# Attention with gated MLP on one core: six heads per Q/K group, matmuls of one kind in pairs, and work moved between engines

## Chip, cores, metric

One core of one Trainium2 chip. The metric is the device time of one execution in microseconds (us), taken as the median of several executions of the same program. The profiles come from one execution each; their spans are about 2 us shorter than the device time.

## The reference

The sequence has 2048 tokens of width 640; there are 32 heads of only 20 columns.

```python
g = sigmoid((x * gate_w).sum(-1, keepdims=True))
# a: full attention
qkv = x @ wqkv                                   # 2048 x 1920
p = softmax(q @ k.T * 20 ** -0.5)                # per head, 2048 x 2048
a = (p @ v).reshape(2048, 640) @ wo
# b: MLP with "mish"
h = x @ w1 + b1                                  # 2048 x 1536
b = (h * tanh(log(1 + exp(h)))) @ w2
out = g * a + (1 - g) * b
```

Inputs, weights and the result are bf16.

## The kernel before

The program is written engine by engine. Each engine works through its own queue and waits on semaphores; an instruction that waits holds up those queued behind it, and this is what the argument turns on: in the run with the multiply on VectorE, the copy of a finished Q product stood behind a multiply that waited 7.12 us.

The first stretch computes V, the gate, Q and K (transposed, `QT` and `KT`) and the whole MLP. A list of events fixes the order: "h" is one hidden tile of the MLP (128 of 1536 features, 512 tokens), "q" and "k" are one Q or K product, "b" is the down-projection of 512 tokens. Q and K come in groups of four heads; each head is padded from 20 to 32 columns, and GpSimd copies the padded weights into `PAD`.

```python
QKP = PB[4]                                      # one PSUM bank for Q and K
# TensorE, for an event "q" or "k":
if qk_last is not None:
    pk, pi = qk_last
    pe.wait_ge(s_qfree if pk == "q" else s_kfree, pi + 1)
for ft in range(NFT):                            # 5 matmuls
    pe.matmul(QKP[:, 0:512], PAD[gb][:, side, ft, :], XT[:, ft, qc*512:(qc+1)*512], ...)
# VectorE:  "q": tensor_copy(QT..., QKP)    4th "h": wait for tanh, multiply HB*UB -> ACTT, four times
# ScalarE:  "k": copy(KT..., QKP)           4th "h": flush_batch(), see below     "b": copy the block out
...
def flush_batch():                               # ScalarE, four tiles
    for t in pending: HB = Identity(h + b1); UB = Exp(h + b1)
    for t in pending: UB = Ln(UB + 1)            # table load before
    for t in pending: UB = Tanh(UB)              # table load before
```

The second part is attention. For each of two halves of the queries (1024 each) it does 512 steps; a step is one head and 128 keys. S is the score product into one of three PSUM buffers `T`, exp moves it to `ETS`, V accumulates into `OTACC`. S matmuls use 128x128 weights. V matmuls use 128x21 weights and put each head of a group of four into its own 32 rows of `OTACC` (a column tile).

```python
ND = 3                                           # buffers T and ETS
# ScalarE
act.wait_ge(s_s, s + 1)
if s >= ND: act.wait_ge(s_v, s - ND + 1)
act.activation(ETS[b], T[b], AF.Exp, scale=SCALE).then_inc(s_e, 1)
# TensorE
def emit_S(s):  # wait s_e >= s-ND+1; two matmuls 128x512 with KTZ (128x128)
def emit_V(s):  # wait s_e >= s+1;   two matmuls 128x512 with V_all (128x21), tile_position=(0, 32*j)
for k0 in range(ND): emit_S(base + k0)
for k in range(steps_per_qr):
    emit_V(base + k)
    if k + ND < steps_per_qr: emit_S(base + k + ND)
```

`KTZ` holds the K rows of one head with all other rows zero, so that S of one head can use all 128 rows of `QT`. After each group of 64 steps VectorE copies `OTACC` out, and the next group's first V waits for that.

The softmax here doesn't subtract the row's maximum and nothing guards it: scores larger than these inputs give would overflow.

Of the kernel before, what the change touches and what calls it, by code (L numbers as in the profile page):

```python
# [10 lines left out]
P = 128  # L11
D = 640
# [3 lines left out]
NG = 8  # L16
NFT = D // P
# [5 lines left out]
def bass_gated_mix__softmax_full_mha__dense_activation_mish__prompt_kernel(  # L23
# [30 lines left out]
    def sem(name):  # L54
        return st.enter_context(nc.semaphore(name))

    V_all = st.enter_context(nc.sbuf_tensor("V_all", [P, NKT, H, 21], BF16))
    QT = st.enter_context(nc.sbuf_tensor("QT", [P, NG, S], BF16))
    KT = st.enter_context(nc.sbuf_tensor("KT", [P, NG, S], BF16))
# [45 lines left out]
    s_ktz = [sem("s_ktz0"), sem("s_ktz1")]  # L105
# [26 lines left out]
    def pool_chain_inc(ins, other=None, other_val=None):  # L132
# [4 lines left out]
        else:  # L137
# [10 lines left out]
    ctxQ = ExitStack()  # L148
    WQKV = ctxQ.enter_context(nc.sbuf_tensor("WQKV", [P, NFT, 1920], BF16, side="right"))
    PAD = [ctxQ.enter_context(nc.sbuf_tensor(f"PAD{i}", [P, 2, NFT, P], BF16, side="right"))  # L150
           for i in range(2)]
# [5 lines left out]
    QKP = PB[4]  # L157
# [5 lines left out]
    items = [(g, qc) for g in range(NG) for qc in range(NQC)]  # L163
# [24 lines left out]
    with nc.Block() as blk:  # L188
        @blk.sync
        def _(sp):  # L190
            for ft in range(NFT):
                sp.dma_start_transpose(XT[:, ft, :], x_ap[:, ft * P:(ft + 1) * P]).then_inc(s_xt, 16)
            sp.dma_start(W1[:, :, :], B_w1.rearrange("(ft p) c -> p ft c", p=P)).then_inc(s_w1, 16)
            sp.wait_ge(s_qfree, NITEMS)
            sp.wait_ge(s_kfree, NITEMS)
# [11 lines left out]
        @blk.vector  # L207
        def _(dve):
            ins = dve.memset(V_all[:, :, :, 0:1], 1.0)
            dve_chain_inc(ins, s_dve_init, 1)  # L210
            dve.wait_ge(s_misc, 16 * N_MISC)
            dve.tensor_copy(B1F[:, :], B1T[:, :]).then_inc(s_b1f, 1)

        @blk.gpsimd
        def _(pool):
            pool.wait_ge(s_wq, 16)
            for g in range(NG):
                b = g % 2
                if g >= 2:
                    pool.wait_ge(s_kready, NQC * (g - 1))  # L220
                pool_chain_wait(pool)
                ins = pool.memset(PAD[b][:, :, :, :], 0.0)
                pool_chain_inc(ins)
                todo = []
                for side in range(2):
                    off = side * D
                    for j in range(4):
                        c0 = off + (4 * g + j) * DH
                        todo.append((side, j, c0))
                for idx, (side, j, c0) in enumerate(todo):  # L230
                    pool_chain_wait(pool)
                    ins = pool.tensor_copy(PAD[b][:, side, :, 32 * j:32 * j + DH],
                                           WQKV[:, :, c0:c0 + DH])
                    if idx == len(todo) - 1:
                        pool_chain_inc(ins, s_pad[b], (g // 2) + 1)
                    else:
                        pool_chain_inc(ins)
# [46 lines left out]
        ctxQ.close()  # L284
        W2 = ctxB.enter_context(nc.sbuf_tensor("W2", [P, NFC, D], BF16, side="right"))

        @blk.sync
        def _(sp):
            sp.dma_start(W2[:, :, :], B_w2.rearrange("(fc p) c -> p fc c", p=P)).then_inc(s_w2, 16)

        @blk.tensor
        def _(pe):
# [4 lines left out]
            for ev in events:  # L297
# [13 lines left out]
                elif kind in ("q", "k"):  # L311
                    i = ev[1]
                    g, qc = items[i]
                    gb = g % 2
                    if qc == 0 and kind == "q":
                        pe.wait_ge(s_pad[gb], (g // 2) + 1)
                    if qk_last is not None:
                        pk, pi = qk_last
                        pe.wait_ge(s_qfree if pk == "q" else s_kfree, pi + 1)
                    side = 0 if kind == "q" else 1  # L320
                    ins = None
                    for ft in range(NFT):
                        ins = pe.matmul(QKP[:, 0:512], PAD[gb][:, side, ft, :],  # L323
                                        XT[:, ft, qc * 512:(qc + 1) * 512],
                                        start=(ft == 0), stop=(ft == NFT - 1))
# [19 lines left out]
        @blk.vector  # L345
        def _(dve):
            pending = []

            def flush_batch():
                for t in pending:  # L350
                    tc, fc = divmod(t, NFC)
                    b = t % BK
                    dve.wait_ge(s_mish_act, t + 1)
                    if fc == 0 and tc >= 2:
                        dve.wait_ge(s_bp_ready, TBC * (tc - 1))
                    dve_chain_wait(dve)
                    ins = dve.tensor_tensor(ACTT[tc % 2][:, fc, :], HB[b][:, :], UB[b][:, :], ALU.mult)  # L357
                    dve_chain_inc(ins, s_act_ready, t + 1)
                pending.clear()

            for ev in events:
                kind = ev[0]
                if kind == "q":
                    i = ev[1]
                    g, qc = items[i]
                    dve.wait_ge(s_qready, i + 1)
                    dve.tensor_copy(QT[:, g, qc * 512:(qc + 1) * 512], QKP[:, 0:512]).then_inc(s_qfree, 1)  # L367
                elif kind == "h":
                    pending.append(ev[1])
                    if len(pending) == BK:  # L370
                        flush_batch()
                elif kind == "b":
                    if pending:
                        flush_batch()
            if pending:
                flush_batch()

        @blk.scalar
        def _(act):
# [25 lines left out]
            for ev in events:  # L405
# [5 lines left out]
                elif kind == "k":  # L411
                    i = ev[1]
                    g, qc = items[i]
                    act.wait_ge(s_kready, i + 1)
                    act.copy(KT[:, g, qc * 512:(qc + 1) * 512], QKP[:, 0:512]).then_inc(s_kfree, 1)  # L415
# [16 lines left out]
    ETS = [ctxC.enter_context(nc.sbuf_tensor(f"ETS{i}", [P, 1024], BF16)) for i in range(3)]  # L432
# [6 lines left out]
    KTZ = [[ctxC.enter_context(nc.sbuf_tensor(f"KTZ{b}_{j}", [P, S], BF16)) for j in range(4)]  # L439
           for b in range(2)]  # L440
    T = [ctxC.enter_context(nc.psum_tensor(f"T{i}", [P, 1024], FP32)) for i in range(3)]
    OTACC = ctxC.enter_context(nc.psum_tensor("OTACC", [P, 1024], FP32))
    ND = 3

    steps = []
    for qr in range(NQR):
        for g in range(NG):
            for j in range(4):
                for kt in range(NKT):
                    steps.append((qr, g, j, kt))  # L450
    NS = len(steps)
    assert NS == NSTEPS
    steps_per_qr = NG * 4 * NKT
    wo_v = A_wo.rearrange("(g j r) c -> j r g c", g=NG, j=4, r=DH)

    with nc.Block() as blk2:
        @blk2.vector
        def _(dve):
# [6 lines left out]
            for b in range(2):  # L465
                for j in range(4):
                    dve_chain_wait(dve)
                    ins = dve.memset(KTZ[b][j][:, :], 0.0)  # L468
                    if b == 1 and j == 3:
                        dve_chain_inc(ins, s_cinit, 1)  # L470
                    else:
                        dve_chain_inc(ins)
# [38 lines left out]
        @blk2.scalar  # L511
        def _(act):
            for s, (qr, g, j, kt) in enumerate(steps):
                b = s % ND
                act.wait_ge(s_s, s + 1)
                if s >= ND:
                    act.wait_ge(s_v, s - ND + 1)
                act.activation(ETS[b][:, :], T[b][:, :], AF.Exp, scale=SCALE).then_inc(s_e, 1)  # L518

        @blk2.sync  # L520
        def _(sp):
# [15 lines left out]
            for gi in range(NGRP):  # L537
                gb = gi % 2
                g = gi % NG
                qr = gi // NG  # L540
                if gi >= 2:
                    sp.wait_ge(s_s, (gi - 1) * STEPS_PER_GROUP)
                for j in range(4):
                    sp.dma_start(KTZ[gb][j][32 * j:32 * j + DH, :],  # L544
                                 KT[32 * j:32 * j + DH, g, :]).then_inc(s_ktz[gb], 16)
                if qr >= 1 and g == 1:
                    out_dmas(qr - 1)
                if gi >= 1:
                    pg = gi - 1
# [14 lines left out]
        def _(pe):  # L564
            def emit_S(s):
                qr, g, j, kt = steps[s]
                b = s % ND
                gi = qr * NG + g
                gb = gi % 2
                if s >= ND:  # L570
                    pe.wait_ge(s_e, s - ND + 1)
                if j == 0 and kt == 0:
                    pe.wait_ge(s_ktz[gb], 16 * 4 * (gi // 2 + 1))
                ins = None
                for c in range(2):
                    q0 = qr * 1024 + c * 512
                    ins = pe.matmul(T[b][:, c * 512:(c + 1) * 512],  # L577
                                    KTZ[gb][j][:, kt * P:(kt + 1) * P],
                                    QT[:, g, q0:q0 + 512],
# [3 lines left out]
            def emit_V(s):  # L583
                qr, g, j, kt = steps[s]
                b = s % ND
                h_ = 4 * g + j
# [5 lines left out]
                for c in range(2):  # L592
                    ins = pe.matmul(OTACC[32 * j:32 * j + DH + 1, c * 512:(c + 1) * 512],  # L593
                                    V_all[:, kt, h_, 0:DH + 1],
                                    ETS[b][:, c * 512:(c + 1) * 512],
# [20 lines left out]
            for qr in range(NQR):  # L616
# [5 lines left out]
                for k in range(steps_per_qr):  # L622
                    s = base + k
                    emit_V(s)
                    if k + ND < steps_per_qr:
                        emit_S(s + ND)
# [32 lines left out]
```

## Time and profile before

| | before |
|---|---|
| median of 6 runs | 1607.46 us (1606.52 to 1612.88) |
| first stretch (last MLP block copied out) | 394.7 us |
| setup of attention, to the first S | 18.7 us |
| first half, first S to end of last V | 556.4 us |
| between the halves | 38.4 us |
| second half | 554.5 us |
| after the last V | 42.1 us |

The windows view gives the busy time of each engine in chosen stretches (columns: us of the stretch, busy us and instruction count of TensorE, its weight loads, VectorE, ScalarE and GpSimd, then the granted clock, which is the share of full speed that TensorE was allowed, the DMA share and GB/s). Of the kernel before:

```profile
core 0: us, PE busy (x) PEld busy (x) DVE busy (x) ACT busy (x) POOL busy (x), PEclk, DMA share, GB/s
48.00:234.00 186.00, 114.20 (x433) 42.34 (x434) 30.25 (x53) 76.50 (x123) 20.05 (x54) 0.84 0.00 0
234.00:395.00 161.00, 93.78 (x512) 44.48 (x510) 12.50 (x29) 92.69 (x158) 0.00 (x0) 0.81 0.04 13
395.00:413.00 18.00, 0.00 (x0) 0.00 (x0) 10.46 (x11) 0.00 (x0) 0.00 (x0) 0.57 0.31 64
413.00:970.00 557.00, 550.12 (x2048) 111.60 (x2048) 59.50 (x22) 524.26 (x512) 0.00 (x0) 1.00 0.09 9
```

Two different limits show. From 48 to 234 us no engine is busy all the time and the granted clock is 0.84: engines wait for one another. From 413 to 970 us TensorE and ScalarE both look almost full, and busy time alone can't tell which one is the bound.

For the first stretch, the timeline of the kernel before (start, duration, engine, line; in brackets the idle time of the engine before it and what ended it):

```profile
88.21 1.25 PE L323 MATMUL PB<-XT,PAD 128*128 128x512 bf16 x5 [0.68 <-ACT KT L415]
89.30 1.24 PE L307 MATMUL PB<-XT,W 128*128 128x512 bf16 x5
89.50 0.69 DVE L367 CAST QT<-PB 128x512 bf16<-128x512 f32 x1 [3.28 <-PE PB L323]
90.38 1.24 PE L323 MATMUL PB<-XT,PAD 128*128 128x512 bf16 x5
91.66 0.59 ACT L415 CAST KT<-PB 128x512 bf16<-128x512 f32 x1 [3.50 <-PE PB L323]
...
92.39 1.24 PE L323 MATMUL PB<-XT,PAD 128*128 128x512 bf16 x5 [0.77 <-ACT KT L415]
```

A product, its copy, the next product: only a hidden tile (L307) hides the copy. It is worse when ScalarE is in a batch of four tiles: the K copies wait behind it, and so does TensorE. The waits view from 48 to 234 us has these sums (waiting engine and line, released by, us in total, times, longest):

```profile
PE PB L323 <- ACT KT L415: 43.2, 16, 8.7
PEld PB L323 <- DVE QT L367: 43.1, 31, 11.7
PE PB L323 <- DVE QT L367: 28.5, 23, 11.2
```

The longest waits, 8.7 and 11.2 us, come near the length of a batch: a batch took 11.6 us (four tiles of Identity and Exp, 1.28 us of table load, 2.19 us of Ln, 1.28 us of table load, 2.19 us of Tanh).

For attention, the timeline of TensorE, kernel before (L577 is S, L593 is V; x2 means two matmuls, and durations are modelled, so read the starts):

```profile
700.41 0.60 PE L577 MATMUL T<-QT,KTZ 128*128 128x512 bf16 x2
700.94 0.60 PE L593 MATMUL OTACC<-ETS,V_all 128*21 128x512 bf16 x2
701.48 0.60 PE L577 MATMUL T<-QT,KTZ 128*128 128x512 bf16 x2
702.01 0.60 PE L593 MATMUL OTACC<-ETS,V_all 128*21 128x512 bf16 x2
```

A step is 1.07 us. The starts of single matmuls in the trace tell more. Where matmuls of one kind follow one another the distance is 0.216 us (median of the Q and K products). Within a step it is 0.226 (S to S), 0.309 (S to V), 0.223 (V to V) and 0.312 us (V to S). Nothing released these matmuls late: the exp that V needs had ended 1.0 us earlier. ScalarE's first three exps, which wait for nothing, start 0.92 and 0.90 us apart, but later exps start 1.07 us apart, each 0.04 us after its S has ended. So TensorE is the bound, and 0.19 us of each step is lost at the two changes of kind (the recorded texts call them changes of the tiling mode, or mode changes).

### The profile page before, as it was taken

The page shows a single profiled execution, that of the slowest core. Times are in us where ns is not written, and L with a number is a line of the kernel's source. Part 1 is how long each engine was busy: PE and PEld are TensorE (multiplying, and loading weights), DVE is VectorE, ACT ScalarE, POOL GpSimd, SP SyncE. Part 2 cuts the span into 40 slices and gives each one's busy share as a digit, 9 for nine tenths or more (in the row PEclk, how much of TensorE's full clock was granted, in tenths as well). Part 3 has the DMA queues.
Part 4 walks back from the last instruction along what each step waited for, and adds up shares of the span by engine and source line. Part 5 has one row for each costly group of instructions (what it writes and reads, how often), then busy time and mean ns, then how long its engine had stood idle before and what let it go on. Part 6 is the DMA issues. An engine that isn't in the chain of part 4 may idle for free.

```text
span 1604.7 us, 14101 instructions
## 1 busy us (share of the span) xinstructions
PE 1371.2 (85%) x5536; PEld 346.5 (22%) x5536; DVE 231.0 (14%) x207; ACT 1218.7 (76%) x1306; POOL 26.9 (2%) x76
## 2 busy tenths in 40 slices
PE   4666645556699999999999995999999999999994
PEld 2322212223121121212112122212121221212112
DVE  2211110101102102020210204110102021020205
ACT  0333352781699999999999991899999999999980
POOL 1011100000000000000000000000000000000000
PEclk9978887788799999999999997999999999999997
DMA  6000001000101011010101102001101010110102
GB/s 176 0 1 1 0 1 49 0 1 9 28 1 15 1 16 15 1 15 1 15 2 14 16 1 31 17 1 16 9 7 15 1 15 1 16 15 1 7 1 40
DMA packets 23755, 22.80 MB, mean 14 GB/s; under 512 B 14856, under 2 KB 19080, under 8 KB 23688
## 3 DMA queue, kind: packets, MB, share of 16 engines
q1 hardware_dynamic: 20584, 19.44, 9.2%
q10 hardware_dynamic: 3104, 2.46, 0.5%
q8 instruction: 43, 0.70, 0.2%
q14 instruction: 24, 0.20, 0.0%
HBM read 7.21 MB, written 2.62 MB: 6 GB/s over the span
## 4 chain that ended last, share of the span: by engine, by line
PE 70%; DVE 3%; DMA 1%; issue 0%; SPq 0%; ACT 0%; DVEq 0%
PE OTACC L593 34%; PE T L577 34%; PE T L610 2%; DVE OUNG L483 1%; DMA BCSB<-RTMP 1%; DVE RTMP L487 1%; PE T L612 0%; DVE KTZ L468 0%; ACT ETS L518 0%; DMA KTZ<-KT 0%; SPq L544 0%; DVE WOG L460 0%; SPq L553 0%; SPq L558 0%; DVE DIFF L501 0%
## 5 line engine op out<-in xcount | busy, mean ns | idle before, releaser
L518 ACT ACTIVATE ETS<-T 128x1024 bf16<-128x1024 f32 x1024 | 1048.1, 1024 | 119.2 <-PE T L577 73.9
L577 PE MATMUL T<-QT,KTZ 128*128 128x512 bf16 x2048 | 620.9, 385 | 20.4 <-DMA KTZ<-KT 19.5
L593 PE MATMUL OTACC<-ETS,V_all 128*21 128x512 bf16 x2048 | 616.0, 383 | 12.7 <-DVE OUNG L483 12.2
L577 PEld LDWEIGHTS T<-QT,KTZ 128*128 128x128 bf16 x2048 | 116.9, 97 | 459.4 <-ACT ETS L518 428.6
L593 PEld LDWEIGHTS OTACC<-ETS,V_all 128*21 128x21 bf16 x2048 | 106.0, 90 | 448.6 <-issue 424.9
L323 PE MATMUL PB<-XT,PAD 128*128 128x512 bf16 x320 | 91.7, 423 | 83.0 <-ACT KT L415 43.2
L483 DVE CAST OUNG<-OTACC 128x1024 bf16<-128x1024 f32 x16 | 19.6, 1225 | 862.1 <-PE OTACC L593 862.1
L487 DVE RECIPROCAL RTMP<-OUNG 128x1024 bf16<-128x1024 bf16 x16 | 104.8, 6553 | 0.6
L415 ACT CAST KT<-PB 128x512 bf16<-128x512 f32 x32 | 18.7, 583 | 112.8 <-PE PB L323 112.8
L339 PE MATMUL PB<-W,ACTT 128*128 128x512 bf16 x192 | 59.7, 408 | 44.0 <-ACT BALL L424 35.0
L307 PE MATMUL PB<-XT,W 128*128 128x512 bf16 x240 | 64.3, 418 | 11.2 <-ACT UB L392 10.8
L610 PE MATMUL T<-WOG,OTN 128*128 128x512 bf16 x128 | 39.2, 411 | 36.0 <-DVE OTN L493 36.0
L323 PEld LDWEIGHTS PB<-XT,PAD 128*128 128x128 bf16 x320 | 30.3, 105 | 138.7 <-DVE QT L367 54.8
L423 ACT CAST BALL<-PB 128x512 bf16<-128x512 f32 x16 | 9.3, 583 | 63.4 <-PE PB L341 63.4
L357 DVE TENSOR_TENSOR ACTT<-HB,UB 128x512 bf16<-128x512 bf16 x48 | 20.4, 425 | 164.9 <-ACT UB L402 161.3
L341 PE MATMUL PB<-W,ACTT 128*128 128x128 bf16 x192 | 44.0, 229 | 0.0
L249 PE MATMUL PB<-WQKV,XT 128*128 128x500 bf16 x80 | 23.7, 393 | 22.0 <-DMA XT<-in_A_x_dram 22.0
L367 DVE CAST QT<-PB 128x512 bf16<-128x512 f32 x32 | 22.1, 691 | 106.7 <-PE PB L323 106.7
L339 PEld LDWEIGHTS PB<-W,ACTT 128*128 128x128 bf16 x192 | 19.9, 104 | 73.7 <-ACT BALL L424 38.0
L307 PEld LDWEIGHTS PB<-XT,W 128*128 128x128 bf16 x240 | 25.3, 107 | 46.5 <-issue 12.4
L391 ACT ACTIVATE HB<-PB,B1F 128x512 bf16<-128x512 f32 x48 | 33.7, 702 | 0.7 <-PE PB L307 0.7
L392 ACT ACTIVATE UB<-PB,B1F 128x512 bf16<-128x512 f32 x48 | 34.0, 708 | 0.0
(35 smaller groups left out, 296.9 us busy)
## 6 DMA issues: line engine op xcount, KB each, us to landing
KTZ<-KT SPq DMA_DIRECT2D x64, 80.0 KB
BCSB<-RTMP SPq DMA_DIRECT2D x64, 64.0 KB, 5.6
W<-in_B_w_dram SPq DMA_DIRECT2D x2, 1920.0 KB, 8.8
out_dram<-OUTT SPq DMA_DIRECT2D x16, 160.0 KB, 1.8
WQKV<-in_A_wqkv_dram ACTq DMA_DIRECT2D x1, 2400.0 KB, 9.5
WOG<-in_A_wo_dram SPq DMA_DIRECT2D x4, 200.0 KB
B1T<-in_B_b_dram ACTq DMA_DIRECT2D x12, 0.2 KB, 7.8
XT<-in_A_x_dram SPq DMA_TRANSPOSE x5, 5.3
```

Source lines behind the costliest of these rows:

```text
L307: ins = pe.matmul(hp[:, 0:TCW], W1[:, ft, fc * P:(fc + 1) * P], XT[:, ft, tc * TCW:(tc + 1) * TCW], start=(ft == 0), stop=(ft == NFT - 1))
L323: ins = pe.matmul(QKP[:, 0:512], PAD[gb][:, side, ft, :], XT[:, ft, qc * 512:(qc + 1) * 512], start=(ft == 0), stop=(ft == NFT - 1))
L339: pe.matmul(BPa[:, 0:512], ACTT[tc % 2][:, fc, tbl * P:(tbl + 1) * P], W2[:, fc, 0:512], start=(fc == 0), stop=(fc == NFC - 1))
L341: ins = pe.matmul(BPb[:, 0:128], ACTT[tc % 2][:, fc, tbl * P:(tbl + 1) * P], W2[:, fc, 512:640], start=(fc == 0), stop=(fc == NFC - 1))
L391: act.activation(HB[b][:, :], hp[:, 0:TCW], AF.Identity, bias=B1F[:, fc:fc + 1], scale=1.0)
L392: act.activation(UB[b][:, :], hp[:, 0:TCW], AF.Exp, bias=B1F[:, fc:fc + 1], scale=1.0).then_inc(s_hp_actdone, 1)
L483: ins = dve.tensor_copy(OUNG[:, :], OTACC[:, :])
L487: ins = dve.reciprocal(RTMP[:, :], OUNG[:, :])
L518: act.activation(ETS[b][:, :], T[b][:, :], AF.Exp, scale=SCALE).then_inc(s_e, 1)
L577: ins = pe.matmul(T[b][:, c * 512:(c + 1) * 512], KTZ[gb][j][:, kt * P:(kt + 1) * P], QT[:, g, q0:q0 + 512], start=True, stop=True)
L593: ins = pe.matmul(OTACC[32 * j:32 * j + DH + 1, c * 512:(c + 1) * 512], V_all[:, kt, h_, 0:DH + 1], ETS[b][:, c * 512:(c + 1) * 512], star ...
L610: pe.matmul(T[b][:, 0:512], OTN[:, g, tbl * P:(tbl + 1) * P], WOG[:, g, 0:512], start=(g == 0), stop=(g == NG - 1))
```

## The change

The intent: Q and K in groups of six heads without padding (fewer products, no `PAD`), separate PSUM banks for Q and K, all Q/K copies on VectorE, the multiply on GpSimd, W2 loaded early; in attention, S and V in pairs with six exp buffers.

```diff
-    QKP = PB[4]
+    QKB = {'q': PB[4], 'k': PB[5]}
...
-                    if qk_last is not None:
-                        pk, pi = qk_last
-                        pe.wait_ge(s_qfree if pk == "q" else s_kfree, pi + 1)
+                    if i >= 1:
+                        pe.wait_ge(s_qfree if kind == "q" else s_kfree, i)
+                    c0 = (0 if kind == "q" else D) + g6 * 6 * DH
...
-                        ins = pe.matmul(QKP[:, 0:512], PAD[gb][:, side, ft, :],
+                        ins = pe.matmul(QKB[kind][0:mc, 0:512], WQKV[:, ft, c0:c0 + mc],
...  # VectorE: both copies, nothing else
-                    dve.tensor_copy(QT[:, g, qc * 512:(qc + 1) * 512], QKP[:, 0:512]).then_inc(s_qfree, 1)
+                    dve.tensor_copy((QT if kind == "q" else KT)[0:mc, g6, qc * 512:(qc + 1) * 512],
+                                    QKB[kind][0:mc, 0:512]).then_inc(s_qfree if kind == "q" else s_kfree, 1)
...  # the multiply, in GpSimd's own queue
-                    ins = dve.tensor_tensor(ACTT[tc % 2][:, fc, :], HB[b][:, :], UB[b][:, :], ALU.mult)
+                pool.tensor_tensor(ACTT[tc % 2][:, fc, :], HB[b][:, :], UB[b][:, :],
+                                   ALU.mult).then_inc(s_act_ready, 1)
...  # ScalarE no longer copies K
-                    act.copy(KT[:, g, qc * 512:(qc + 1) * 512], QKP[:, 0:512]).then_inc(s_kfree, 1)
...  # attention: 6 instead of 8 zeroed KTZ, one K load per head; six ETS
-                if s >= ND:
-                    act.wait_ge(s_v, s - ND + 1)
+                if s >= NE:                      # NE = 6
+                    act.wait_ge(s_v, s - NE + 1)
...
-                for k in range(steps_per_qr):
-                    s = base + k
-                    emit_V(s)
-                    if k + ND < steps_per_qr:
-                        emit_S(s + ND)
+                for k in range(0, steps_per_qr, 2):
+                    for kk in (k, k + 1):
+                        if kk + ND < steps_per_qr:
+                            emit_S(base + kk + ND)
+                    for kk in (k, k + 1):
+                        emit_V(base + kk)
```

(Cut: the zeroing of the unused rows of `QT` and `KT`, the index arithmetic of the six-head groups, the K loads, the W2 load.)

## The prediction

> What bounds the kernel now. The windows view and the timeline show three stretches: projections and MLP, 0 to 395 us; setup to the first score matmul at 413.4 us; attention, twice 512 steps of S (2 matmuls), exp, V (2 matmuls), each half followed by about 40 us of normalisation, output projection and store.
>
> Attention is bound by TensorE, not by ScalarE's exp. A step lasts 1.070 us: its matmuls start 0.226 (S to S), 0.309 (S to V), 0.223 (V to V) and 0.312 us (V to S) apart. Between matmuls of one kind (end of the first half; MLP) it is 0.216, so each change between 128x128 and 128x21 matmuls costs about 0.095 us. [...] ScalarE's first three exps, which wait for nothing, start 0.91 us apart; later each starts 0.04 us after its S ends.
>
> The first stretch is bound by a serial chain through one PSUM bank: each Q or K product waits for the copy of the one before (0.69 us on VectorE, 0.59 on ScalarE), and the K copies stand in ScalarE's queue behind a four-tile exp/ln/tanh batch (11.6 us). So 24 hidden tiles take 48 to 248 us, at a granted clock near 0.8.
>
> What the change does.
>
> 1. S,S,V,V order halves the mode changes. Two steps: 2 x 0.31 + 2 x 0.225 + 4 x 0.216 = 1.935 us, 0.967 a step. Saving 0.103 x 1024 = 105 us. Six exp buffers let V lag; exp at 0.91 just fits.
> 2. At the 14 group boundaries inside the halves V waits 0.94 us for the copy of OTACC; one more S pair covers 0.44 of it: 6 us.
> 3. Six heads per Q/K group: 48 products, not 64; separate banks for Q and K; all copies on VectorE; no padding. TensorE should run without waits: 24 x 3 x 1.08 us = 78 us, not 200. ScalarE's 11.6 us a batch fits in TensorE's 13.
> 4. W2 is loaded early: the 9 us wait before the first down-projection goes, but ScalarE's last batch (about 8 us) is exposed instead. First evacuated block at about 135, not 262.6 us; the same 4.28 us cadence; the stretch ends near 270.
> 5. The gating multiply moves to GpSimd. [...] ScalarE reuses a tile each 1.14 us: 0 to 4 us lost.
> 6. Setup: six zeroed KTZ, not eight (2.4 us); first S waits for one copy, not four (about 2 us).
>
> Sum: 125 + 4 + 105 + 6 = 240 us off 1607, plus 3 for a cold clock: 1370 us. Range 1345 to 1398. Faster by over 2%: 0.97; within 2%: 0.02; slower: 0.01.
>
> Signs. Right: S to V and V to S still 0.31 but half as many, step mean 0.967, TensorE never waiting for exp; clock near 1.0 from 48 to 126 us; first evacuated MLP block at 135; attention from 284. Wrong on 1: steps near 1.07, or exps back to back with TensorE waiting for them. Wrong on 3: gaps before Q/K products released by VectorE copies, or tiles waiting for ScalarE.
>
> What could make it wrong: exp in steady state slower than 0.91 us with its second semaphore wait; a multiply on GpSimd over 1.3 us, stalling ScalarE each batch; a clock that stays low in the first stretch; KTZ loads late behind other waits of their queue.

## The result and the profile after

The changed kernel's median is 1365.16 us (8 runs, 1361.86 to 1367.38); the kernel before ran at 1608.64 us (16 runs). The ratio is 0.848, with a 95% interval of 0.8468 to 0.8492. A ratio here is the mean time of one kernel's fast runs over that of the other's fast runs of the same rounds, so not quite the ratio of the medians.

| us, from the traces | before | after | saved | predicted |
|---|---|---|---|---|
| first stretch, to the last MLP block copied out | 394.7 | 271.2 | 123.5 | 125, less 3 for a cold clock |
| setup, to the first S | 18.7 | 14.1 | 4.6 | 4 |
| both halves of attention | 1110.9 | 998.9 | 112.0 | 105 + 6 |
| between and after the halves | 80.5 | 81.2 | -0.7 | 0 |
| span | 1604.7 | 1365.4 | 239.3 | 237 |

(A "cold clock" is a stretch in which TensorE, after a wait, runs below full speed. In the kernel before, after the wait of 9.02 us for W2, a 512-column matmul took 0.43 us to the next start from 257.7 to 260.8 us, and 0.216 from 261.3 us on. That block took 6.15 us to the start of the next one, the later ones 4.28; the predicted 3 us are the author's estimate.) The windows view of the changed kernel:

```profile
48.00:127.00 79.00, 78.63 (x427) 42.82 (x424) 32.99 (x50) 62.77 (x98) 22.46 (x20) 1.00 0.00 1
127.00:271.00 144.00, 94.79 (x513) 45.35 (x511) 1.37 (x2) 88.90 (x152) 31.36 (x28) 0.83 0.00 1
271.00:285.00 14.00, 0.00 (x0) 0.00 (x0) 8.63 (x9) 0.21 (x2) 0.00 (x0) 0.63 0.34 67
285.00:785.00 500.00, 496.65 (x2048) 153.78 (x2048) 59.29 (x21) 494.45 (x512) 0.00 (x0) 1.00 0.11 10
```

The Q/K part is now TensorE work without gaps, 78.63 of 79 us, at full clock. The timeline of the changed kernel there (L299 is a Q or K product, L286 a hidden tile, L329 the copies, L340 the multiply):

```profile
90.12 2.32 PE L299 MATMUL PB<-XT,WQKV 128*120 128x512 bf16 x10
...
91.40 0.69 DVE L329 CAST QT<-PB 120x512 bf16<-120x512 f32 x1 [1.47 <-PE PB L299]
...
92.28 1.24 PE L286 MATMUL PB<-XT,W 128*128 128x512 bf16 x5
92.48 0.69 DVE L329 CAST KT<-PB 120x512 bf16<-120x512 f32 x1 [0.39 <-PE PB L299]
...
93.36 2.32 PE L299 MATMUL PB<-XT,WQKV 128*120 128x512 bf16 x10
93.87 4.49 POOL L340 TENSOR_TENSOR ACTT<-HB,UB 128x512 bf16<-128x512 bf16 x4 [8.45 <-ACT UB L367]
```

A Q and a K product follow each other without a gap (x10), no PE line has a wait in brackets, and the copies and the multiply run beside them. The waits view from 48 to 127 us has no wait of TensorE for a copy any more; the waits that remain are those of engines with time to spare:

```profile
DVE QT L329 <- PE PB L299: 34.8, 23, 2.0
ACT HB L356 <- PE PB L286: 14.1, 9, 2.0
```

TensorE in attention, changed kernel (L545 is S, L562 is V):

```profile
501.24 1.03 PE L562 MATMUL OTACC<-ETS,V_all 128*21 128x512 bf16 x4
502.20 1.04 PE L545 MATMUL T<-QT,KTZ 128*128 128x512 bf16 x4
503.17 1.03 PE L562 MATMUL OTACC<-ETS,V_all 128*21 128x512 bf16 x4
```

Four of a kind, and 1.93 us from one V to the next V for two steps. The distances between starts of single matmuls, from the traces (median us, and how many pairs):

```
            S to S         S to V         V to V         V to S
before      0.226 (1028)   0.309 (1020)   0.223 (1028)   0.312 (1019)
after       0.216 (1538)   0.309 (510)    0.216 (1538)   0.312 (509)
```

The price of a change is the same; there are half as many. At the 14 group boundaries inside the halves the S to V distance was 1.25 us before and is 0.82 us now: the copy of `OTACC` takes 1.225 us in both traces, but two S pairs cover more of it.

### The profile page after: what moved, and what is told of

The parts are those of the page before. It is cut to its first block, busy times and chain, and to the rows that moved or that the text cites. A ratio compares the mean times of both kernels' runs of the same rounds, so it can differ in the third digit from the quotient of the medians.

```text
span 1365.4 us, 13841 instructions
## 1 busy us (share of the span) xinstructions
PE 1230.3 (90%) x5456; PEld 430.8 (32%) x5456; DVE 232.0 (17%) x177; ACT 1141.9 (84%) x1274; POOL 54.0 (4%) x52
## 4 chain that ended last, share of the span: by engine, by line
PE 74%; DVE 4%; DMA 2%; issue 0%; SPq 0%; ACT 0%; DVEq 0%; ACTq 0%
PE OTACC L562 36%; PE T L545 35%; PE T L579 2%; DVE OUNG L452 1%; DMA BCSB<-RTMP 1%; DVE RTMP L456 1%; PE T L581 0%; DVE KTZ L437 0%; DMA out_dram<-OUTT 0%; DVE OUTT L475 0%; DMA KTZ<-KT 0%; DVE DIFF L470 0%; DVE WOG L430 0%; SPq L521 0%; SPq L526 0%
## 5 line engine op out<-in xcount | busy, mean ns | idle before, releaser
L487 ACT ACTIVATE ETS<-T 128x1024 bf16<-128x1024 f32 x1024 | 988.8, 1022 | 62.4 <-PE T L545 62.4
L545 PE MATMUL T<-QT,KTZ 128*128 128x512 bf16 x2048 | 532.5, 383 | 16.7 <-DMA KTZ<-KT 14.9
L562 PE MATMUL OTACC<-ETS,V_all 128*21 128x512 bf16 x2048 | 528.6, 381 | 6.1 <-DVE OUNG L452 6.1
L545 PEld LDWEIGHTS T<-QT,KTZ 128*128 128x128 bf16 x2048 | 158.7, 98 | 358.4 <-ACT ETS L487 212.1
L562 PEld LDWEIGHTS OTACC<-ETS,V_all 128*21 128x21 bf16 x2048 | 148.4, 92 | 349.2 <-ACT ETS L487 214.0
L286 PE MATMUL PB<-XT,W 128*128 128x512 bf16 x240 | 60.5, 400 | 11.2 <-ACT UB L357 10.8
L340 POOL TENSOR_TENSOR ACTT<-HB,UB 128x512 bf16<-128x512 bf16 x48 | 53.8, 1153 | 186.7 <-ACT UB L367 186.7
L299 PE MATMUL PB<-XT,WQKV 128*120 128x512 bf16 (+1 forms) x240 | 55.8, 379 | 0.0
L299 PEld LDWEIGHTS PB<-XT,WQKV 128*120 128x120 bf16 (+1 forms) x240 | 30.3, 127 | 22.7 <-issue 1.7
L286 PEld LDWEIGHTS PB<-XT,W 128*128 128x128 bf16 x240 | 23.9, 102 | 42.6 <-ACT UB L357 11.8
L462 DVE TENSOR_TENSOR OTN<-OUNG,BCSB 128x1024 bf16<-128x1024 bf16 x16 | 11.1, 692 | 154.2 <-DMA BCSB<-RTMP 154.2
```

The costliest lines, as they stand in the source:

```text
L286: ins = pe.matmul(hp[:, 0:TCW], W1[:, ft, fc * P:(fc + 1) * P], XT[:, ft, tc * TCW:(tc + 1) * TCW], start=(ft == 0), stop=(ft == NFT - 1))
L299: ins = pe.matmul(QKB[kind][0:mc, 0:512], WQKV[:, ft, c0:c0 + mc], XT[:, ft, qc * 512:(qc + 1) * 512], start=(ft == 0), stop=(ft == NFT - 1))
L340: pool.tensor_tensor(ACTT[tc % 2][:, fc, :], HB[b][:, :], UB[b][:, :], ALU.mult).then_inc(s_act_ready, 1)
L487: act.activation(ETS[s % NE][:, :], T[b][:, :], AF.Exp, scale=SCALE).then_inc(s_e, 1)
L545: ins = pe.matmul(T[b][:, c * 512:(c + 1) * 512], KTZ[j6][:, kt * P:(kt + 1) * P], QT[:, g6, q0:q0 + 512], start=True, stop=True)
L562: ins = pe.matmul(OTACC[32 * j:32 * j + DH + 1, c * 512:(c + 1) * 512], V_all[:, kt, h, 0:DH + 1], ETS[s % NE][:, c * 512:(c + 1) * 512], ...
```

## Experiments

The theory, A: a change between S and V matmuls costs TensorE about 0.095 us, whatever else happens; the first stretch was a chain of waits made by one shared bank together with copies and multiplies queued behind work they have nothing to do with. Rivals: B, the six exp buffers brought the attention gain; C, the cost between S and V comes from new weights, operands and PSUM banks, not from the change between wide and narrow weights; D, the shared bank alone explains the first stretch. Each kernel was timed in three rounds against the kernel before, whose median in these rounds was 1608.4 to 1608.6 us.

### The old order in the changed kernel

```diff
-  S(k+3), S(k+4), V(k), V(k+1)      # per two steps
+  V(k), S(k+3)                      # per step
```

> The changed kernel with the old order V,S in attention, all else (six exp buffers included) kept. Theory A (each change between S and V matmuls costs TensorE about 0.095 us): the step goes back from 0.967 to 1.070 us and the group stall from 0.51 to 0.94 us, so about +111 us, 1476 us. Rival B (the six exp buffers brought the gain, because exp had been held by the V of three steps before): the step stays near 0.967, 1365 us.

Measured: 1476.73 us, ratio 0.9185 (0.9169 to 0.9200). The exps start 1.070 us apart, S to V is 0.309 and 1.25 us at the boundaries, as in the kernel before. B falls: with six buffers and the old order nothing of the attention gain is left.

### Three exp buffers, new order kept

```diff
-    NE = 6
+    NE = 3      # and three ETS
```

> The changed kernel with three exp buffers instead of six, new order S,S,V,V kept. Theory A with its side condition: V now ends late in each round, exp s needs the buffer of V s-3, and a ring exp - S - V - exp closes; worked out from the measured pieces (exp 1.02, S 0.23, S to V 0.31, V pair 0.60, three hand-overs of about 0.04) a round of two steps takes about 2.24 us, 1.12 a step, about 1520 us: slower than the old order. If the order alone mattered it would stay at 1365 us. Rival B in its simple form (three buffers is what the old step of 1.07 came from) expects about 1476 us.

Measured: 1550.34 us, ratio 0.9647 (0.9630 to 0.9664). The ring is there, and slower than worked out: 2.31 us for two steps, not 2.24. TensorE's timeline in this kernel:

```profile
501.05 0.60 PE L545 MATMUL T<-QT,KTZ 128*128 128x512 bf16 x2 [0.21 <-ACT ETS L487]
501.58 1.03 PE L562 MATMUL OTACC<-ETS,V_all 128*21 128x512 bf16 x4
502.55 0.60 PE L545 MATMUL T<-QT,KTZ 128*128 128x512 bf16 x2
503.36 0.61 PE L545 MATMUL T<-QT,KTZ 128*128 128x512 bf16 x2 [0.21 <-ACT ETS L487]
```

and ScalarE's:

```profile
502.28 1.94 ACT L487 ACTIVATE ETS<-T 128x1024 bf16<-128x1024 f32 x2 [0.38 <-PE OTACC L562]
```

The second S of a round waits for an exp, and the first exp of a round waits for a V. The mistake in my sum was in the hand-overs. From the end of exp to the S it releases took 0.055 us, and from the end of V to the exp it releases 0.097 us, where I had put 0.04 for each. That exp has two semaphores to wait for, and the wait for V stands in the traces of the kernels before and after as an instruction of its own (EVENT_SEMAPHORE, 17 ns); that this makes the difference was not tested. (The expectation names three hand-overs, but its sum of 2.24 us holds two, and the ring has these two.) The new order needs the extra buffers, although the buffers gain nothing on their own.

### Four exp buffers

```diff
-    NE = 6
+    NE = 4      # and four ETS
```

> The changed kernel with four exp buffers. Theory A: exp needs the V of four steps back; the second exp of a round may start about 0.06 us late, still inside its slack, so the step stays 0.967 us and the time 1365 us within 5. If every buffer brought its share (rival B), it would lie between the six and the three buffer kernels.

Measured: 1366.31 us, ratio 0.8490 (0.8477 to 0.8503), the same as with six. One more buffer than before was enough; the step is 0.967 us in this trace too.

### The new attention order in the kernel before

```diff
-  V(k), S(k+3); three ETS
+  S(k+3), S(k+4), V(k), V(k+1); six ETS      # nothing else changed
```

> The kernel before with only the new attention order S,S,V,V and six exp buffers; first stretch and four-head groups as before. Theory A: the attention gain does not depend on the packing of heads: 105 us from the steps and 6 us at group boundaries, so 1608 - 111 = 1497 us. If part of the attention gain came from the six-head packing or its later K loads, less is gained here.

Measured: 1496.46 us, ratio 0.9305 (0.9291 to 0.9319): 112 us gained, the same 112 that were lost when the order was undone in the changed kernel. The attention gain depends neither on the packing of heads nor on the first stretch.

### V with full-width weights (wrong result)

In the kernel before, each V takes 128 weight columns and writes all 128 rows of `OTACC`. The result is useless; the number of matmuls, their operands' tensors, the order and the waits stay.

```diff
-   OTACC[32*j:32*j+DH+1, ...], V_all[:, kt, h_, 0:DH+1], ..., tile_position=(0, 32*j)
+   OTACC[:, ...], <128 neighbouring columns of V_all[:, kt]>, ...
```

> The kernel before with one edit: each V matmul takes 128 weight columns instead of 21 and writes all 128 rows of OTACC (result wrong on purpose). Order V,S and three exp buffers stay. Theory A (it is the change of the tiling mode that costs): all matmul starts are 0.216 us apart when ready, TensorE needs 0.863 us a step, exp becomes the bound at about 0.92 us a step, so about 1608 - 150 = 1455 us. Rival C (the 0.095 us come from changing weights, operands or PSUM banks between S and V, whatever the width): 0.31 us stays and the time stays 1608 us.

Measured: 1448.38 us, ratio 0.8999 (0.8971 to 0.9028). TensorE's timeline:

```profile
500.22 0.59 PE L577 MATMUL T<-QT,KTZ 128*128 128x512 bf16 x2
500.69 0.61 PE L593 MATMUL OTACC<-ETS,V_all 128*128 128x512 bf16 x2
501.14 0.59 PE L577 MATMUL T<-QT,KTZ 128*128 128x512 bf16 x2
501.61 0.61 PE L593 MATMUL OTACC<-ETS,V_all 128*128 128x512 bf16 x2
```

V to S is 0.216 us, down from 0.312, although weights, operands and banks change as before: C falls. S to V is 0.258 us, because V now waits for exp. The exps start 0.904 us apart, back to back, so ScalarE is the bound: V starts 0.056 us after its own exp has ended, where it was 1.0 us in the kernel before. I had taken 0.92 us for the exp, which is the main reason why the sum came out 7 us too high.

The changed kernel holds a second proof, in its trace. In the Q/K part, hidden tiles (128 weight columns) and Q/K products (120 columns) follow each other at 0.216 us, new weights and new bank included. The last Q/K group has only two heads, 40 columns, and there the same changes take 0.309 and 0.312 us. Narrow matmuls that follow one another are 0.216 us apart in the same trace, new weights included, so it is the change between the two forms that costs. What TensorE does at the change the traces do not show; they show only the price.

### One bank for Q and K

```diff
-    QKB = {'q': PB[4], 'k': PB[5]}      # each waits for its own last copy
+    QKB = {'q': PB[4], 'k': PB[4]}      # each waits for the copy of the product before
```

> The changed kernel with Q and K products sharing one PSUM bank again; the copies stay on VectorE. Each K product waits for the copy of the Q product before it; the next Q product is covered by a hidden tile. As measured before, a product after a waited-for copy starts 2.03 us after the last one instead of 1.08: +0.95 x 24 = 23 us, 1388 us. Rival D (the shared bank alone was what made the old stretch 200 us instead of 78): +100 us or more.

Measured: 1386.65 us, ratio 0.8612 (0.8591 to 0.8633): 21.5 us. Batches of four tiles start 16.93 us apart instead of 12.95. D falls: alone, the shared bank costs a sixth of what the first stretch gained.

### K copies on ScalarE

```diff
-  VectorE copies K
+  ScalarE copies K, in the old event order (behind flush_batch)
```

> The changed kernel with the K copies back on ScalarE in the old event order; two banks kept. K products stop while ScalarE works through a four-tile batch. I work out a batch of 20.6 us instead of 12.95 (PE gets five products done, then waits for the end of the batch): +46 us, 1411 us. Gaps before K products released by ScalarE copies, granted clock down. Rival D expects little change.

Measured: 1417.45 us, ratio 0.8801 (0.8779 to 0.8823): 52 us, 6 more than worked out. The waits view from 62 to 126 us:

```profile
DVE QT L329 <- PE PB L299: 58.0, 11, 13.1
...
PE PB L299 <- ACT KT L381: 22.1, 3, 7.4
```

Three waits of up to 7.4 us for a copy that itself takes 0.59 us. Batches after the first took 22.0 to 23.5 us, not 20.6. I had worked with matmuls at full clock; the granted clock is 0.82 from 48 to 126 us here and was 1.00 in the changed kernel. After the longest wait, 7.38 us, the first matmuls start 0.43 us apart instead of 0.216: the next ten took 3.93 us (72.06 to 75.99 us) instead of 2.16. By these starts that wait cost its length and 1.8 us more.

### The multiply on VectorE

```diff
-  GpSimd multiplies, in a queue of its own
+  VectorE multiplies at every fourth "h", between the Q and K copies
```

> The changed kernel with the gating multiply back on VectorE in the old event order, between the Q and K copies. VectorE then waits for a batch's tanh with copies behind it: a batch of about 19.5 us instead of 12.95, +39 us, 1404 us. If the multiply were moved only for its speed, VectorE (0.425 us) would make it no slower, or faster.

Measured: 1405.87 us, ratio 0.8733 (0.8712 to 0.8754): 41 us lost with the faster engine. The timeline:

```profile
66.71 1.98 DVE L332 TENSOR_TENSOR ACTT<-HB,UB 128x512 bf16<-128x512 bf16 x4 [7.12 <-ACT UB L377]
...
68.61 0.68 DVE L342 CAST QT<-PB 120x512 bf16<-120x512 f32 x1
...
69.35 4.52 PE L299 MATMUL PB<-XT,WQKV 128*120 128x512 bf16 x10 [6.17 <-DVE QT L342]
```

VectorE stood for 7.12 us at the multiply, waiting for Tanh, with a finished Q product queued behind it, and TensorE stood for 6.17 us in turn. On GpSimd the multiply takes 1.15 us instead of 0.43 and costs nothing: ScalarE's batches, when nothing else limits them, are 11.64 us apart in the changed kernel and were 11.62 before.

### All three undone together

```diff
-    two banks; VectorE copies K; GpSimd multiplies
+    one bank; ScalarE copies K; VectorE multiplies      # the three edits above
```

> The changed kernel with all three undone together (one bank, K copies on ScalarE, multiply on VectorE), 48 products and early W2 kept. The old trace's batches with two products a tile took 28.65 us: six of them 172 us instead of 78, so +94 us, 1459 us. Of the old kernel's 1476 us with new attention this leaves about 28 us for the 16 products fewer and 9 for the early W2.

(One number in this expectation is a slip: the old kernel with new attention was expected at 1497 us, and the 28 and 9 us follow from that number, not from 1476.)

Measured: 1459.20 us, ratio 0.9073 (0.9060 to 0.9087). This is 94.0 us over the changed kernel, as expected; the three parts alone summed to 114, so they overlap. It leaves 37 us to the kernel before with new attention (1496.46). Two traces show where these lie: 22.1 us between the start of the first hidden tile and the end of the last Q/K product (201.1 against 179.0), 9.4 us from there to the first block copied out, where TensorE waited 9.1 us for W2 before, and 4.6 us in the setup. By these traces the early W2 brought the 9 us expected of it; of the 28 us put down to the products, 22.1 lie there and 4.6 in the setup. The early W2 and the smaller setup were not run on their own.

### Sixty-four products

```diff
-  for ft in range(NFT)                                         # 48 products
+  for r in range(2 if i % 3 == 0 else 1): for ft in range(NFT) # every third twice
```

> The changed kernel with every third Q and K product computed twice, 64 product times instead of 48; nothing else. If TensorE bounds this stretch now, 16 x 1.08 = 17 us are added, 1382 us. If ScalarE (11.6 us a batch) were the bound, part of it would hide.

Measured: 1382.76 us, ratio 0.8590 (0.8574 to 0.8606): 17.6 us for 16 product times. Nothing hides, so TensorE does bound that part of the changed kernel.

### Threes instead of pairs

```diff
-                for k in range(0, steps_per_qr, 2): ...                    # S S V V
+                sizes = ([3] * 20 + [2, 2]) * (steps_per_qr // STEPS_PER_GROUP)   # S S S V V V
```

> The changed kernel with threes instead of pairs: S,S,S,V,V,V (20 threes and two pairs per group of 64 steps). Theory A: 2 x 0.31 + 2 x 0.225 + 8 x 0.216 = 2.80 us per three, 0.936 a step on average, 32 us; three S pairs also cover the group boundary wait, 7 us more: 1326 us. If exp is really slower than 0.935 us in steady state it becomes the bound: then 1335 us or more and TensorE waits for exp.

Measured: 1320.92 us, ratio 0.8217 (0.8198 to 0.8236), result correct. The price per change stays 0.309 and 0.312 us, with 350 and 349 of them. The 5 us beyond the expectation are a sum of two things that I had not expected. Where a three crosses from one head to the next, the V matmuls of the two heads go to different column tiles, and they ran at the same time:

```profile
420.19 0.81 PE L545 MATMUL T<-QT,KTZ 128*128 128x512 bf16 x3
420.94 1.04 PE L562 MATMUL OTACC<-ETS,V_all 128*21 128x512 bf16 x6
```

The merged line hides it: six V matmuls span 1.04 us where four span 1.03. In the trace the starts are 420.936, 420.942, 421.158 and 421.165 us. There are 64 such starts, 5 to 15 ns after the one before, so 64 x 0.216 = 14 us saved. By their semaphores, the first two of the four starts are the first matmuls of the two heads and the last two the second ones: the later head's first matmul started before the earlier head's second, which stands ahead of it in the queue. Some 10 us are given back: 32 S starts come 0.3 us late, because S has caught up with exp.

### Threes, and the MLP's blocks copied out by VectorE

```diff
-    BPa = PB[6]; BPb = PB[7]                    # ScalarE copies each block
+    BPa = [PB[6], PB[4]]; BPb = [PB[7], PB[5]]  # VectorE copies, two pairs in turn
```

> The one before, and the down-projection's blocks are copied out by VectorE (idle there) from two pairs of PSUM banks in turn, instead of by ScalarE from one pair. ScalarE no longer waits 54 us for these blocks and TensorE no longer waits 0.85 us after each: I expect the MLP to end near 235 us instead of 271, so 1290 us (1280 to 1305).

Measured: 1287.82 us, ratio 0.8005 (0.7993 to 0.8017), result correct. The MLP ends at 232 us instead of 268 in the run before (271 in the trace of the changed kernel). This is the fastest version. Its exps start 0.92 us apart in the median and 0.932 us in the mean within a half, and alone they would need 0.90 to 0.92: TensorE and ScalarE are now nearly even, so another order of S and V has little left to give.

## Why the prediction was right

The time, 1365.16 us, lies 5 us from the predicted 1370 and inside the range. Since a sum can be right by luck, each term was held against its own measurement.

1. Fewer mode changes, 105 us, and the group boundaries, 6 us: measured 112.0 us in the traces, 111.6 by undoing the order in the changed kernel and 112.1 by adding it to the kernel before. That the cause is the change between full-width and narrow matmuls, and not new weights, is shown by the full-width V and by the 40-column products.
2. Extra buffers only let V lag: shown. Six buffers with the old order gain nothing, three with the new order cost 185 us, four are as good as six.
3. The chain in the first stretch, 78 us instead of 200 for 24 hidden tiles and their Q/K products: 78.6 us, from 50.2 to 128.8, to the end of the last product, where the kernel before took 200.1, from 48.1 to 248.2. (The last hidden tile itself ended at 126.5 and, before, at 233.6.) The chain itself is worth 94 us, shown by undoing three parts together, and no single part explains it (21.5, 52 and 41 us).
4. The first block at 135 us: 134.75 us. The end near 270 us: 271.2 us. The wait that replaced the one for W2 came as predicted, and so did the cold clock: the second block followed 7.17 us after the first, the later two at 4.28 us. That these 3 us came is partly luck. In this trace the first matmul of the second block started 3.58 us after the last one of the first block, and then a 512-column matmul took 0.427 us to the next start. The runs with the old order and with three exp buffers change nothing in this stretch, and their traces have the same 3.58 us; but there it took 0.216 us, the second block followed after 4.25 and 4.28 us, and the stretch ended at 265.6 and 265.0 us. This term rests on traces alone.
5. The multiply on GpSimd, 0 to 4 us lost, which was the author's estimate and shown by no trace at the time: 1.15 us a tile in the trace of the changed kernel, and no loss.
6. Setup, 4 us: 4.6 us, from the traces alone.

What was off were sizes in the experiments: the hand-overs in the ring of three buffers (0.055 and 0.097 us, not 0.04; 30 us on that kernel), the cold clock after ScalarE's batches (the 6 us are put down to it), the pace of unhindered exps (0.904 us in the median, not 0.92; most of the 7 us), and the simultaneous V matmuls (not thought of).

## What to carry to other kernels

Two engines that both look almost full (TensorE 99% and ScalarE 94% busy in attention here) need not be equally the bound: compare the start-to-start distance of an instruction where it waits for nothing (exp: 0.91 us) with its distance in steady state (1.07 us). An instruction was as late here as the slowest thing ahead of it in its queue (a Q copy behind a multiply that waited 7.12 us), so put an evacuation that another engine waits for where nothing ahead of it can wait long, even if the displaced work then runs on a slower engine (1.15 us instead of 0.43). And when matmuls of two shapes alternate and each change costs 0.095 us as here, run several of one shape in a row and give the buffers between them one slot more (1366.31 us with four exp buffers, 1550.34 with three).
